# A four-tap convolution on two halves of TensorE's rows: no shifted copies of k, and another listed order

## The chip, the cores and the metric

The kernel runs on one core of a Trainium2 chip. A core has TensorE (PE, with its weight loads as PEld), VectorE (DVE), ScalarE (ACT), GpSimd (POOL) and SyncE (SP), and 16 DMA engines. The metric is the device time of one execution in microseconds (us), taken as the median of several.

## The reference

All tensors have 2048 rows (time) and 640 columns (channels), in bf16. Part A is a long convolution with gates, part B a feed-forward network:

```python
k_shift = sum over t in 0..3 of k_pad[:, t:t + S, :] * shift_k[:, 3 - t]   # short convolution, 4 taps per channel
kv = k_shift * v
y = irfft(rfft(kv, 2S) * rfft(ssm_k, 2S))[:S] + kv * ssm_D                 # long convolution, per channel
h = x + layernorm(x) * y
out = h + (silu(layernorm(h) @ w_gate) * (layernorm(h) @ w_up)) @ w_down   # inner width 1728
```

The short convolution is what the change is about: each output of a channel is the sum of the current and the three rows before of `k`, each times a number of that channel.

## The kernel before

Time is cut into four blocks of 512 rows. Row `t` of a block lies on partition `t // 4` at slot `r = t % 4`. For each block `j` the stages, with the names that the plan gives them, are: `kj` (short convolution, times v, gives `kv`), `gj` (the block of `ssm_k` turned), `Gj` and `Xj` (spectra of `g` and `kv`: matmuls of line 388, taken out of PSUM by ACT or DVE at lines 377 and 380, sums on DVE at 423 and 452 to 464), `mij` (complex products on DVE, 789 to 818), `nj` and `ij` (layernorm sums on ACT at 829 and 876; inverse transform, matmuls of line 960, and the gate on DVE), `tj` (the second layernorm, turned to `hT`), and `fj` (the feed-forward network: gate and up projections, matmuls of line 1184 into 128 x 512 outputs, then the down projection, line 1077).

The last 64 of the 1728 inner columns are the `tail`: `last_chunk` (1089) multiplies 64 partitions at a time, alternating between partitions 0 to 63 and 64 to 127.

The short convolution is done by matmuls whose stationary operand is a 128-channel slab of turned `k` (channels on partitions, time along it), and whose moving operand is a diagonal matrix of tap values; their sum over the taps is the output with time on partitions.

- Block 0: `k` is loaded plainly, turned by TensorE (629, taken out at 633) into four arrays by slot, and multiplied with 128-wide diagonals `diag`, one for each tap and slab: 80 matmuls of 128 columns (661).
- Blocks 1 to 3: `load_two` (565) loads `k` turned by DMA (576) into half of the tile `T`. Three more moves (`put`, 580; each of 64 partitions, by ACT at 584 or by DMA at 582) build arrangements in which partitions 64 to 127 hold the same 64 channels as partitions 0 to 63, moved in time. So one 128-row matmul with a 64-wide pair of stacked diagonals (`pairs`) does two taps of 64 channels: 80 matmuls of 64 columns a block (670).
- The taps are turned by TensorE (1341, 1358). DVE and POOL fill `diag` (1349), POOL fills `pairs` (1371).
- An output is taken out of PSUM slot by slot, four times a block: by DVE straight with the product by v (680), or by ACT (686) with DVE's product after it (687).

The program's order is written out by hand. Every operation is numbered as it is added to a plan; `ORDER` (77) lists the numbers. Each engine, and each DMA queue (SP's and POOL's), does its operations in that order. A negative number `-n-1` takes the other way given for operation `n`: an eviction or a product on DVE in place of ACT, or a sum by an accumulating DMA from POOL's queue (`add_into`, 284, and `or_add`, 289, which records line 292) in place of DVE. `SLOTS` gives the number of buffers of each kind; one buffer of `ps` is a pair of PSUM banks, and there are four for all uses. `spin` (1328) puts matmuls with no use in front of work to come.

Of the kernel before, what the change touches and what calls it, by code (L numbers as in the profile page):

```python
# [17 lines left out]
D = 640  # L18
# [53 lines left out]
TWOTAPS = True  # L72
TWONS = 640
# [147 lines left out]
def kernel(ctx: ExitStack, tc: tile.TileContext, A_q, A_k, A_v, A_shift_k, A_ssm_k, A_ssm_D, B_x,  # L221
# [90 lines left out]
    WF = fixed([P, R, 4, P], BF16, "WF")  # L312
    WI = fixed([P, 4, R, P], BF16, "WI")
    taps = fixed([P, 4 * KT], FP32, "taps")
    diag = new("diag") if TWOTAPS else fixed([P, KT * 4, P], BF16, "diag")
    if TWOTAPS:
        T = fixed([P, 2 * KT * TW], BF16, "T")
        taps2 = fixed([P, 4 * KT], FP32, "taps2")
# [219 lines left out]
    def window_of(gT, prev):  # L538
# [22 lines left out]
        return H  # L561

    H2 = P // 2

    def load_two(j):

        t = tk
# [961 lines left out]
```

## Time and profile before

| what | us |
|---|---|
| median of 3 executions | 258.9 (258.63 to 259.22) |
| the profiled execution | 258.74 |
| its span in the profile | 257.0 |
| PE busy | 248.3 |
| DVE busy | 199.8 |
| ACT busy | 176.8 |
| POOL busy | 74.0 |

The profile's span begins and ends a little inside the execution. The granted clock of TensorE is full in all slices. A matmul's duration in a row is longer than its spacing in a row of matmuls, since they are pipelined; spacings are taken from the chain of waits (pieces of work and their time) or from merged rows of the timeline (start, time, engine, line, operation, count).

### The profile page before, as it was taken

To read this page: it belongs to the slowest core of one execution; us is meant where nothing else is said; L and a number is where in the kernel's file an instruction comes from. 1 tells how busy PE (TensorE), PEld (TensorE's weight loads), DVE (VectorE), ACT (ScalarE), POOL (GpSimd) and SP (SyncE) were. 2 spreads that over 40 slices of the span, in tenths; PEclk is the share of its full clock that TensorE was granted. 3 is DMA by queue.
4 is the path that set the end of the run, shared out by engine and by line. 5 is a ranking of instruction groups with operands and counts; after the bars stand their busy time and mean duration, and the time that the engine had idled before them with its cause. 6 is when DMAs were issued, how large, how long until landed. Compare 5 with 4: busy or idle time off the path is not lost.

```text
span 257.0 us, 4668 instructions
## 1 busy us (share of the span) xinstructions
PE 248.3 (97%) x1802; PEld 149.8 (58%) x1802; DVE 199.8 (78%) x283; ACT 176.8 (69%) x297; POOL 74.0 (29%) x98
## 2 busy tenths in 40 slices
PE   7899997999999999999999999999999999999994
PEld 7786765654444876664445776544456754444662
DVE  3889999999999999999999999999999300001313
ACT  2499999977997995884586987976687244452400
POOL 5864105111111303427014211369940023000000
PEclk9999999999999999999999999999999999999999
DMA  6999999899896898999997989969690317000002
GB/s 215 379 213 281 264 212 353 205 189 261 196 182 220 139 235 131 191 218 194 192 238 134 219 202 143 218 149 211 172 270 4 77 26 101 3 0 0 0 28 77
DMA packets 54720, 43.31 MB, mean 169 GB/s; under 512 B 25605, under 2 KB 48970, under 8 KB 54698
## 3 DMA queue, kind: packets, MB, share of 16 engines
q1 hardware_dynamic: 48000, 28.58, 44.6%
q0 software_dynamic: 6688, 14.43, 30.7%
q8 instruction: 14, 0.23, 0.4%
q14 instruction: 8, 0.07, 0.1%
q10 hardware_dynamic: 10, 0.01, 0.0%
HBM read 23.99 MB, written 4.59 MB: 111 GB/s over the span
## 4 chain that ended last, share of the span: by engine, by line
PE 80%; ACT 9%; DMA 3%; DVE 3%; issue 2%; SPq 1%; POOL 0%; ACTq 0%; DVEq 0%
PE ps L1184 45%; PE ps L1077 23%; PE ps L388 5%; PE ps L960 4%; DMA big<-in_A_q_dram 3%; ACT big L377 2%; PE ps L670 2%; ACT row L829 2%; ACT row L876 2%; ACT S L377 1%; ACT big L488 1%; DVE row L971 1%; DVE big L974 1%; DVE big L687 0%; ACT big L686 0%
## 5 line engine op out<-in xcount | busy, mean ns | idle before, releaser
L1184 PE MATMUL ps<-big,big 128*128 128x512 bf16 x540 | 118.4, 379 | 0.0
L1184 PEld LDWEIGHTS <-big 128*128 128x128 bf16 x540 | 52.8, 98 | 62.2 <-issue 0.4
L1077 PE MATMUL ps<-wd,tT 128*128 128x320 bf16 (+2 forms) x416 | 59.0, 299 | 0.0
L1077 PEld LDWEIGHTS <-tT 128*128 128x128 bf16 x416 | 40.2, 98 | 16.9 <-issue 1.3
L1176 ACT ACTIVATE tT<-ps 128x1024 bf16<-128x1024 f32 x24 | 24.6, 1025 | 21.5 <-PE ps L1184 21.3
L388 PE MATMUL ps<-big,WF 128*128 128x320 bf16 x224 | 36.7, 298 | 1.2 <-ACT big L377 0.7
L817 DVE TENSOR_TENSOR big<-S,S 128x2560 bf16<-128x2560 bf16 x24 | 35.3, 1490 | 0.0
L1174 ACT CAST co<-ps 128x1024 bf16<-128x1024 f32 x24 | 23.8, 1010 | 11.9 <-PE ps L1184 11.6
L388 PEld LDWEIGHTS <-WF 128*128 128x128 bf16 x224 | 21.2, 97 | 11.5 <-issue 2.8
L292 POOL DMA_DIRECT2D S<-big x11 | 13.9, 1263 | 48.3 <-DVE big L817 15.4
L1178 DVE TENSOR_TENSOR tT<-tT,co 128x2048 bf16<-128x2048 bf16 x12 | 14.5, 1223 | 15.7 <-ACT co L1174 15.7
L818 DVE TENSOR_TENSOR S<-S,big 128x2560 bf16<-128x2560 bf16 x17 | 25.2, 1488 | 0.1
L829 ACT ACTIVATE row<-big 128x640 bf16<-128x640 bf16 x32 | 23.4, 740 | 1.1 <-DMA big<-in_A_q_dram 0.6
L887 ACT ACTIVATE row<-big,sm 128x640 bf16<-128x640 bf16 x22 | 19.6, 924 | 3.0 <-DVE sm L865 3.0
L1113 POOL DMA_DIRECT2D out_dram<-row x12 | 13.0, 1530 | 25.7 <-ACT row L1112 25.7
L1196 DVE TENSOR_TENSOR tT<-tT,co 128x512 bf16<-128x512 bf16 x4 | 1.7, 424 | 21.7 <-ACT co L1195 21.7
L377 ACT CAST S<-ps 128x640 bf16<-128x640 f32 (+1 forms) x27 | 15.0, 613 | 1.3 <-PE ps L388 1.3
L1112 ACT CAST row<-ps 128x640 bf16<-128x640 f32 x12 | 7.8, 696 | 10.0 <-PE ps L1077 8.9
L377 ACT ACTIVATE big<-ps 128x640 bf16<-128x640 f32 (+1 forms) x26 | 14.7, 617 | 0.0
L582 POOL DMA_DIRECT2D T<-T x5 | 5.2, 1039 | 25.5 <-DMA T<-in_A_k_dram 10.0
L851 POOL TENSOR_TENSOR sm<-sm 128x4 f32<-128x4 f32 x4 | 7.2, 1790 | 18.4 <-ACT row L876 18.4
L789 DVE TENSOR_TENSOR big<-S,S 128x2560 bf16<-128x2560 bf16 (+1 forms) x10 | 12.2, 1224 | 0.0
(111 smaller groups left out, 316.7 us busy)
## 6 DMA issues: line engine op xcount, KB each, us to landing
S<-big POOLq DMA_DIRECT2D x9, 640.0 KB, 6.6
big<-in_B_w_gate_dram SPq DMA_DIRECT2D x14, 320.0 KB, 5.3
big<-in_B_w_up_dram SPq DMA_DIRECT2D x11, 320.0 KB, 4.8
big<-in_A_ssm_k_dram SPq DMA_DIRECT2D x4, 640.0 KB, 5.7
big<-in_A_q_dram SPq DMA_DIRECT2D x4, 640.0 KB, 7.1
big<-in_A_v_dram SPq DMA_DIRECT2D x4, 640.0 KB, 6.1
wd<-in_B_w_down_dram SPq DMA_DIRECT2D x1, 2080.0 KB, 11.8
out_dram<-big SPq DMA_DIRECT2D x3, 640.0 KB, 3.4
```

Of the source, the lines that this page charges most:

```text
L292: op.other = ("add", P * n * 2 / 1280 * plan.TOOK[1280] / 16 * 2.1, lambda: nc.gpsimd.dma_start(out=to(), in_=what(), accum_op=ALU.add, ma ...
L377: (lambda: nc.scalar.activation(dst(), src(), ACT.Copy, scale=2.0)) if twice else (lambda: nc.scalar.copy(dst(), src())),
L388: nc.tensor.matmul(ap(ps)[:, h, 0:NH], w, ap(src)[:, r, h * NH:(h + 1) * NH], start=(first and i == 0), stop=(last and i == len(rs) - 1), ...
L817: dve(1490, lambda b=b, xs=xs, hs=hs: nc.vector.tensor_mul(flat2(b), X.part(xs), H.part(hs)), [X.at(xs), H.at(hs)], [b], [A.b])
L818: dve(1490, lambda b=b, dst=dst, f=f: f(A.part(dst), A.part(dst), flat2(b)), [b], [A.at(dst)])
L829: act(825, lambda r=r, junk=junk: nc.scalar.activation(ap(junk), ap(x)[:, r, :], ACT.Square, scale=D ** -0.5, accum_out=sm(s, 1)[:, r:r + ...
L887: nc.scalar.activation(ap(row), ap(x)[:, r, :], ACT.Identity, bias=sm(s, 5)[:, r:r + 1], scale=sm(s, 4)[:, r:r + 1])
L1077: nc.tensor.matmul(to, t, w, skip_group_check=True, **flags)
L1174: act(1010, lambda ps=ps: nc.scalar.copy(ap(co)[:, at:at + 2, :], ap(ps)), src, [(co, gi % 2)])
L1176: act(1010, lambda ps=ps: nc.scalar.activation(ap(tT)[:, c:c + 2, :], ap(ps), ACT.Silu), src, [done(range(c, c + 2), ROWS)])
L1178: dve(1220, lambda: nc.vector.tensor_mul(ap(tT)[:, c - 2:c + 2, :], ap(tT)[:, c - 2:c + 2, :], ap(co)), [co], [done(range(c - 2, c + 2), R ...
L1184: nc.tensor.matmul(ap(ps)[:, i, :], ap(w)[:, k, off:off + P], ap(hT)[:, k, :], start=(k == 0), stop=(k == KT - 1))
```

## The change

All four blocks now take one way, `by_halves`:

- `T` holds one turned copy of `k`, five slabs of 512 times with a pad of 16 in front. The three times before a block are copied there by POOL. Blocks 1 to 3 are loaded by the same four DMA transposes a block (`load_rows`). Block 0 is loaded to a buffer of its own (one more `big` buffer), turned by TensorE as before, and its evictions write every fourth element of `T`.
- The 64-wide diagonals now carry one tap: `pairs[p, t, c, e]` is the tap `t` of channel `128 c + p` where `p % 64 == e`, and zero elsewhere. All are made by one DVE product; one POOL addition makes the two stacked identities. The tiles `diag` and `taps2`, their fills and the second turning of the taps are gone, and so are all `put` moves.
- A block has three groups: slabs 0 and 1, slabs 2 and 3, slab 4. For each time offset `at` from -3 to 3 and each slab there are two matmuls, one on partitions 0 to 63 and one on 64 to 127, into two PSUM banks. The stationary operand is a strided window of `T`; the moving operand holds the diagonals of all slots to which this window contributes: 256 columns for `at = 0`, 192, 128 and 64 columns for 1, 2 and 3 steps away. This makes 14 matmuls and 2048 columns a slab, 70 matmuls and 10240 columns a block.
- An output is taken out group by group, three times a block, of 1024, 1024 and 512 columns; DVE's product by v follows in the same cut. The transforms of line 388 wait for column groups of `kv` instead of slots.

`ORDER` is new throughout. What it lists, decoded by counting the operations:

- First loads on SP's queue: before WF, g0, k0, x0, (a tail of w_down), v0; now (that tail), k0, g0, x0, v0, WF.
- On TensorE ahead of the first projection of `f0`: before 24 of the 32 matmuls of `X1` (line 388), with the other 8 behind the first two projections; now all 32. Of the removed setup's two spins of four matmuls, one now stands ahead of `f0` and one ahead of `X2`.
- On ACT ahead of the last step of `t0`: the layernorm sums `n1` (8 rows of lines 829 and 876) are now behind it. Evictions for DVE and ACT are dealt out anew.
- Convolutions: block 2 has its groups in three places apart (ahead of `i1`, ahead of the down projection of `f0`, in it); block 3 in two places.
- the 32 matmuls of `X2` are now followed at once by the 32 of `G3`, between `f0` and `f1`; before, `X2` lay among the last chunks of `f0`, and two projections of `f1` stood between.
- Three sums that were on DVE (two of 128 x 2560, one of 128 x 640) become accumulating DMAs.

```diff
+    if TAPROWS:
+        T = fixed([P, KT * TW], BF16, "T")
+        ident2 = fixed([P, P // 2], BF16, "ident2")
+        pairs = fixed([P, 4 * KT, P // 2], BF16, "pairs")
...
+    def load_rows(j):
+        plan.add("pool", 500, lambda: nc.gpsimd.tensor_copy(tk()[:, :, PAD - 3:PAD], tk()[:, :, TW - 3:TW]), [of_t(*[(R - 1, r) for r in range(1, R)])], [of_t("halo")])
+        for a in range(R):
+            transfer(MB / 4, lambda a=a: nc.sync.dma_start(
+                out=tk()[:, :, PAD + a * P:PAD + (a + 1) * P], in_=kk[j * BLK + a * P:j * BLK + (a + 1) * P, :], transpose=True),
+                [], [of_t(*[(a, r) for r in range(R)])])
...
+    def by_halves(kv, v, behind):
+        for i in range(3):
+            cs = range(2 * i, min(2 * i + 2, KT))
+            ps = conv_ps()
+            def mm(cs=cs, ps=ps):
+                for at in (0, 1, -1, 2, -2, 3, -3):
+                    r0, r1 = max(0, at), min(R - 1, R - 1 + at)
+                    for c in cs:
+                        for b in range(2):
+                            rows = slice(b * H2, b * H2 + H2)
+                            nc.tensor.matmul(ap(ps)[:, b, 0:len(cs) * R * H2].rearrange("p (r c e) -> p r c e", r=R, e=H2)[:, r0:r1 + 1, c - cs[0], :], tk()[rows, c, PAD + at:PAD + at + BLK - 3:R],
+                                             ap(pairs).rearrange("p (t c) e -> p t c e", c=KT)[rows, r0 - at:r1 - at + 1, c, :],
+                                             start=(at == 0), stop=(abs(at) > 1), skip_group_check=True)
...
+            op = plan.add("act", 1010 if n > 1 else 590, lambda to=to, src=src: nc.scalar.copy(to(), src()), [ps, v], [(kv, f"w{i}")], (),
+                          ("dve", 1230 if n > 1 else 690, straight))
+            op.rest = (dve(690 if n > 1 else 420, lambda cols=cols: nc.vector.tensor_mul(cols(ap(kv)), cols(ap(kv)), cols(rd(v))), [v], [(kv, f"w{i}")]),)
...
+    if TAPROWS:
+        plan.add("pool", 350, lambda: nc.gpsimd.tensor_tensor(ap(ident2), ap(ident)[:, 0:P // 2], ap(ident)[:, P // 2:P], op=ALU.add), [ident], [ident2])
+        dve(1480, lambda: nc.vector.tensor_mul(ap(pairs), ap(ident2).unsqueeze(1).broadcast_to([P, 4 * KT, P // 2]), ap(taps).unsqueeze(2).broadcast_to([P, 4 * KT, P // 2])), [ident2, taps], [pairs])
+    for _ in range(SPINS[0] if TAPROWS else 0):
+        spin(4)
-SLOTS = {'S': 8, 'big': 12, 'kT': 0, 'tT': 1, 'row': 5, 'sg': 0, 'co': 2, 'ps': 4, 'sm': 6}
+SLOTS = {'S': 8, 'big': 13, 'kT': 0, 'tT': 1, 'row': 5, 'sg': 0, 'co': 2, 'ps': 4, 'sm': 6}
```

More of the change, by code (lines that the diff above doesn't have):

```diff
@@ L72 @@
 TWOTAPS = True
+TAPROWS = True
 TWONS = 640
@@ L314, with tk @@
     taps = fixed([P, 4 * KT], FP32, "taps")
-    diag = new("diag") if TWOTAPS else fixed([P, KT * 4, P], BF16, "diag")
-    if TWOTAPS:
+    if TAPROWS:
+        T = fixed([P, KT * TW], BF16, "T")
+        ident2 = fixed([P, P // 2], BF16, "ident2")
+        pairs = fixed([P, 4 * KT, P // 2], BF16, "pairs")
+        def tk():
+            return ap(T).rearrange("p (c t) -> p c t", c=KT)
+        TOKENS = tuple((a, r) for a in range(R) for r in range(R))
+    else:
+        diag = new("diag") if TWOTAPS else fixed([P, KT * 4, P], BF16, "diag")
+    if TWOTAPS and not TAPROWS:
         T = fixed([P, 2 * KT * TW], BF16, "T")
@@ L389, in mm @@
                                      start=(first and i == 0), stop=(last and i == len(rs) - 1), skip_group_check=True)
-        pe(136 * len(ws) * len(rs), mm, [(src, x) for r in rs for x in (r, f"{r}w", f"{r}n")] + [WF] + ([(m, "f")] if m else []) + ([] if first else [ps]), [ps], holds)
+        pe(136 * len(ws) * len(rs), mm, [(src, x) for r in rs for x in (r, f"{r}w", f"{r}n")] + [(src, f"w{i}") for i in range(ws[0], ws[-1] + 2)] + [WF] + ([(m, "f")] if m else []) + ([] if first else [ps]), [ps], holds)
     def wide(n, ws):
@@ L621, in turned_k @@
             return k
-        src = rd if plan.block else plain
+        src = rd if plan.block or TAPROWS else plain
         kT = T if TWOTAPS else new("kT")
@@ L633, in turned_k @@
             evict(lambda copy, r=r, pt=pt: copy(
-                tk0()[:, :, r, 1:] if TWOTAPS else ap(kT)[:, :, r, PAD:], turned(pt)[:, 0:D].rearrange("p (c t) -> p c t", c=KT)),
-                [pt], [of_t(("K", r)) if TWOTAPS else (kT, r)], other=490)
+                tk()[:, :, PAD + r:PAD + r + BLK - 3:R] if TAPROWS else tk0()[:, :, r, 1:] if TWOTAPS else ap(kT)[:, :, r, PAD:], turned(pt)[:, 0:D].rearrange("p (c t) -> p c t", c=KT)),
+                [pt], [of_t(*[(a, r) for a in range(R)]) if TAPROWS else of_t(("K", r)) if TWOTAPS else (kT, r)], other=490)
             if table:
@@ L640, in kv_of @@
     def kv_of(j, kT, before, v, behind=None):
+        if TAPROWS:
+            if j == 0:
+                dve(60, lambda: nc.vector.memset(tk()[:, :, PAD - 3:PAD], 0.0), [], [of_t("halo")])
+            kv = new("t4")
+            by_halves(kv, v, behind)
+            return kv
         two_taps = TWOTAPS and j > 0
@@ L690, in kv_of, with src, cols, to @@
         return kv
+    def by_halves(kv, v, behind):
[11 more added lines that the diff above has]
+                                             start=(at == 0), stop=(abs(at) > 1), skip_group_check=True)
+            n = len(cs)
+            op = pe(530 * n + 190, mm, [of_t("halo", *TOKENS), pairs], [ps], [kv], 258)
+            if behind:
+                op.deps.add(behind)
+            def src(ps=ps, n=n):
+                return ap(ps)[:, :, 0:n * R * H2].rearrange("p b (r c e) -> p r c b e", r=R, e=H2)
+            def cols(t, cs=cs):
+                return t[:, :, cs[0] * P:(cs[-1] + 1) * P]
+            def to(cols=cols):
+                return cols(ap(kv)).rearrange("p r (c b e) -> p r c b e", b=2, e=H2)
+            def straight(to=to, src=src, cols=cols):
+                nc.vector.tensor_mul(to(), src(), cols(rd(v)).rearrange("p r (c b e) -> p r c b e", b=2, e=H2))
+            op = plan.add("act", 1010 if n > 1 else 590, lambda to=to, src=src: nc.scalar.copy(to(), src()), [ps, v], [(kv, f"w{i}")], (),
+                          ("dve", 1230 if n > 1 else 690, straight))
+            op.rest = (dve(690 if n > 1 else 420, lambda cols=cols: nc.vector.tensor_mul(cols(ap(kv)), cols(ap(kv)), cols(rd(v))), [v], [(kv, f"w{i}")]),)
     def by_rows(kv, v):
@@ L1345 @@
     dve(170, lambda: nc.vector.tensor_copy(ap(taps), ap(pt)[:, 0, 0:4 * KT]), [pt], [taps])
-    for c in range(KT):
+    if TAPROWS:
+        plan.add("pool", 350, lambda: nc.gpsimd.tensor_tensor(ap(ident2), ap(ident)[:, 0:P // 2], ap(ident)[:, P // 2:P], op=ALU.add), [ident], [ident2])
+        dve(1480, lambda: nc.vector.tensor_mul(ap(pairs), ap(ident2).unsqueeze(1).broadcast_to([P, 4 * KT, P // 2]), ap(taps).unsqueeze(2).broadcast_to([P, 4 * KT, P // 2])), [ident2, taps], [pairs])
+    for c in () if TAPROWS else range(KT):
         def fill(c=c, v=nc.vector if c < DIAGDVE else nc.gpsimd):
@@ L1367 @@
     fills = []
-    for c in range(KT if TWOTAPS else 0):
+    for c in range(KT if TWOTAPS and not TAPROWS else 0):
         def fill2(c=c):
```

6 lines of the change are left out of this document (4 added, 2 removed), and 77 rows, old and new, of the table ORDER.

## The prediction

> **What bounds the kernel now.** The page's first lines, then its chain of waits in order of time (start, us, what).
>
> ```profile
> span 257.0 us, 4668 instructions
> PE 248.3 (97%) x1802; PEld 149.8 (58%) x1802; DVE 199.8 (78%) x283; ACT 176.8 (69%) x297; POOL 74.0 (29%) x98
> ...
> 50.07 0.44 PE ps L1020 x5
> 50.51 2.17 PE ps L388 x16
> 52.68 2.16 PE ps L1184 x10
> 54.84 1.09 PE ps L388 x8
> ...
> 103.07 0.29 PE ps L388 x2
> ...
> 103.98 0.69 ACT row L1112
> ...
> 143.52 2.63 PE ps L670 x80
> ...
> 253.67 0.42 DVE row L1123
> ```
>
> From 50.07 on the chain is matmuls to the end, but for 1.3 us from 103.36 to 104.67. So what follows the first projection at 52.68 is worth its time on PE: 253.67 - 52.68 = 200.99 us. Ahead of it, another thing rules. The windows (us, then busy time and count of PE, PEld, DVE, ACT, POOL, granted clock, DMA share):
>
> ```profile
> 8.94:51.68 42.74, 39.67 (x434) 30.08 (x435) 40.89 (x79) 41.40 (x95) 16.97 (x34) 1.00 1.06 265
> 50.07:253.67 203.60, 203.28 (x1305) 114.64 (x1304) 156.11 (x187) 135.38 (x203) 51.78 (x51) 1.00 0.70 146
> ```
>
> In 8.94 to 51.68 ACT and DVE are busy for 41.40 and 40.89 of 42.74 us, and the 434 matmuls there are worth some 36 us at their spacings (some 168 of 320 columns at 0.136 us, 186 of 128 at 0.056, 80 of 64 at 0.033, from rows here and below): PE waits for evictions and sums. So I cost the change twice: the start by the work of ACT and DVE and by when they can begin, the rest by PE's work alone.
>
> **The convolution on PE.** A row of 80 old matmuls of 64 columns takes 2.63 us, 32.9 ns each. The other spacings, and the only matmuls that already run on half of the rows, from the timeline and the groups:
>
> ```profile
> 13.56 2.40 PE L661 MATMUL ps<-big,T 128*128 128x128 bf16 x40
> ...
> 89.11 12.12 PE L1077 MATMUL ps<-wd,tT 128*128 128x320 bf16 x88
> 101.16 0.72 PE L1077 MATMUL ps<-wd,tail 64*128 64x320 bf16 x8
> 101.81 1.26 PE L1077 MATMUL ps<-wd,tT 128*128 128x320 bf16 x8
> ...
> L661 PE MATMUL ps<-big,T 128*128 128x128 bf16 x80 | 5.0, 219 | 0.0
> L1077 PEld LDWEIGHTS <-tail 64*128 64x128 bf16 x32 | 1.2, 94 | 1.6 <-issue 1.3
> ```
>
> 128 columns: (2.40 - 0.219) / 39 = 56 ns. 320 columns: (12.12 - 0.30) / 87 = 136 ns. The tail's eight matmuls of 320 columns, on rows 0 to 63 and 64 to 127 in turn, take 101.81 - 101.16 = 0.65 us; one after another they would take 1.09, in pairs 0.54. So the halves run side by side, and going in and out of them costs: 12.70 us from 89.11 to 101.81, less 88 x 0.136 and 4 x 0.136, leaves 0.19.
>
> A pair then costs what one matmul of its width does. Between 2.5 ns and the column time (56 at 128, 136 at 320: 0.417 ns a column), 256 columns cost 109 ns, 192 83, 128 56, and 64 take the measured 33. A slab: 109 + 2 x (83 + 56 + 33) = 453 ns; five slabs 2.26 us. Block 2 has three visits: 2.26 + 3 x 0.19 = 2.83. Block 3 has two: 2.64. Together 5.47 against 2 x 2.63: **+0.2 us**. If the narrow pairs are held by two loads of 33 ns each (66 for 128 and 64 columns), a slab costs 539 ns and the sum is +1.1. If the halves didn't overlap at all, 5 x 2 x 453 = 4.53 a block and +4.7. I take +0.2, since the tail is the nearest row.
>
> The Trainium skill ("TensorE: Matmul & The Clock Gate", section "The mechanism") speaks against it: a weight load goes ahead of a running matmul only where the row groups differ. Read strictly, each pair would wait for its load; the tail's eight in 0.65 us don't show that. What it would make here is the third rival.
>
> The spin of four matmuls now ahead of `X2` costs 4 x 56 ns: **+0.2 us**. Eight matmuls of line 388 that stood behind the start of `f0` now stand ahead of it: **-1.1 us** (the chain's 1.09 at 54.84).
>
> **The start.** When data comes, and what ACT and DVE can do then:
>
> ```profile
> 0.80 0.35 SPq L1386 DMA_DIRECT2D WF<-const_wf  x1
> 1.20 0.50 SPq L343 DMA_DIRECT2D big<-in_A_ssm_k_dram  x1
> 1.75 0.52 SPq L616 DMA_DIRECT2D T<-in_A_k_dram  x1
> 2.31 0.59 SPq L355 DMA_DIRECT2D big<-in_A_q_dram  x1
> ...
> 7.06 0.75 PE L486 MATMUL ps<-ident,big 128*128 128x128 bf16 x10 [1.11 <-DMA big<-in_A_ssm_k_dram]
> 8.94 0.69 ACT L488 COPY big<-ps 128x640 bf16<-128x640 bf16 x1 [0.73 <-PE ps L486]
> 8.98 1.12 PEld L629 LDWEIGHTS <-T 128*128 128x128 bf16 x20 [0.24 <-DMA T<-in_A_k_dram]
> 11.30 0.74 ACT L829 ACTIVATE row<-big 128x640 bf16<-128x640 bf16 x1 [0.57 <-DMA big<-in_A_q_dram]
> 12.03 0.72 ACT L876 ACTIVATE row<-big 128x640 bf16<-128x640 bf16 x1
> 17.65 0.82 DVE L680 TENSOR_TENSOR big<-ps,big 128x640 bf16<-128x640 f32 x1
> 49.53 0.49 DVE L1022 COPY big<-ps 128x640 bf16<-128x640 bf16 x1
> 50.32 1.36 ACT L1022 COPY big<-ps 128x640 bf16<-128x640 bf16 x2
> ```
>
> Before, WF (512 KB) is first, and g0, k0 and x0 (640 KB each) are there at 7.0, 9.0 and 11.3: some 2 us for 640 KB. With WF sixth, k0 lands at about 5.8, g0 at 7.5, x0 at 9.6, v0 at 11.7, WF at 13.4 (estimates at that rate). ACT then takes out three pieces of k0 (0.69 each) from 6.3 to 8.4, and five rows of `n0` (0.72 apart) from 9.6 to 13.2, 5.7 us of work by 13.4; before, it had done two evictions and three rows, 3.5 us. It is **2.2 to 2.5 us ahead**, and waits little for the late WF.
>
> What ACT has to do ahead of `hT` stays nearly the same. By the lists: eight rows of `n1` less (-5.8), two k0 evictions more and one of g0 less (+0.7), three halves of spectra (half of 0.705 each, +1.1), two of g1 and g2 (+1.4), three of `X1` (+2.1), the kv of block 1 as 1010 + 1010 + 586 ns instead of three of 700 (+0.5), `t0` as four evictions instead of two and one row of L887 (+0.4); sum +0.4. The rows:
>
> ```profile
> L1174 ACT CAST co<-ps 128x1024 bf16<-128x1024 f32 x24 | 23.8, 1010 | 11.9 <-PE ps L1184 11.6
> L1195 ACT CAST co<-ps 128x512 bf16<-128x512 f32 x4 | 2.3, 586 | 4.1 <-PE ps L1184 4.1
> L686 ACT CAST big<-ps 128x640 bf16<-128x640 f32 x10 | 6.8, 705 | 0.0
> L887 ACT ACTIVATE row<-big,sm 128x640 bf16<-128x640 bf16 x22 | 19.6, 924 | 3.0 <-DVE sm L865 3.0
> L680 DVE TENSOR_TENSOR big<-ps,big 128x640 bf16<-128x640 f32 x6 | 4.9, 824 | 0.9 <-PE ps L661 0.7 <-ACT S L377 0.2
> L687 DVE TENSOR_TENSOR big<-big,big 128x640 bf16<-128x640 bf16 x10 | 4.7, 484 | 0.0
> L380 DVE TENSOR_SCALAR big<-ps 128x320 bf16<-128x320 f32 x6 | 2.8, 480 | 0.0
> L423 DVE TENSOR_TENSOR S<-big,S 128x2560 bf16<-128x2560 bf16 x3 | 4.5, 1491 | 0.0
> L1349 DVE TENSOR_SCALAR big<-ident,taps 128x128 bf16<-128x128 bf16 x16 | 3.2, 295 | 0.1
> L584 ACT COPY T<-T 64x2570 bf16<-64x2570 bf16 x3 | 7.0, 2332 | 0.1
> ```
>
> DVE: its 16 fills go (3.2 us), and one product of 1280 elements comes. The trace has none; the bounds are 0.97 (twice 484, L687) and 1.65 (twice 824, L680). I take 1.5, nearer L680, since one operand is fp32; it runs at about 7 to 8.5 ahead of g0's evictions. kv of block 0 is taken out by DVE in pieces of 1024, 1024 and 512: with 824 for 640, 1.29 ns an element bounds it above, 1.32 + 1.32 + 0.66 = 3.3, as much as the four old ones. v0 at 11.7 lets it end at about 15; before, the last one ended at 18.47. From there to the last step of `t0` DVE took 49.53 + 0.49 - 18.47 = 31.55. Its list for this stretch now has four halves of spectra more (L380, +1.9), the sum of `G2` (L423, +1.5), two evictions of g less (-1.0), block 1 as three products (some 0.7 + 0.7 + 0.4) instead of one L680 and three L687 (-0.5), and four rows of `t0` for three and two evictions (-0.5): +1.4. So it is done at 15 + 33.0 = 48.0. A turn and one eviction by ACT (0.45 and 0.69) make `hT` whole at 49.1; before, 50.32 + 1.36 = 51.68. That is -2.6, and ACT's side says -2.2 to -2.5. Last, `f0` stood 1.0 behind `hT` for 16 matmuls of `X1`; now one transform (0.54) follows the last turn. The start of `f0` moves from 52.68 to about 49.7: **-3.0 us**, bounds 0 and -5 (when DVE and ACT both gain what they save and wait for nothing).
>
> Costs that lie under others: evictions of k0 that write every fourth element (0.49 on DVE; 0.82 if they run as L680 does; one is on DVE's list, under the wait for g0); POOL's addition and halo copies, in place of 24 fills and five moves (POOL is busy for 29%); DMA transposes of k for block 1 behind the convolution of block 0 (at about 13 instead of 10.31), while the convolution of block 1 came at 40.58. SP's loads for `f0` queue behind them, three of 0.5 to 1.4 us.
>
> **The rest.** ACT loses 7.0 us of copies and gets `n1` (5.8) where it was busy for 135 of 204 us; DVE loses three sums to POOL's queue, which loses five of T's moves. These buy nothing on PE. `X2` and `G3` in one run hold 64 matmuls, 8.7 us, with 13 evictions on ACT (9.2 us at L686's 0.705) and one of L1112 ahead of them: PE waits 0.5 to 1.5 us there, about the 1.3 at 103.4 that it replaces. The step on DVE that closes the kernel is the same.
>
> **Sum.** 258.74 (profiled) - 3.0 - 1.1 + 0.2 + 0.2 = 255.0; the median lies 0.16 above the profiled execution: 255.2.
>
> **Rivals.**
> 1. The start isn't freed: ACT and DVE wait at 9 to 14 for WF and v0, or for the order. `f0` starts at 52.7 as before, and only -1.1 + 0.4 is left: 258.2. For it: DMA's share is 1.06 in 8.94 to 51.68, so loads may come later than at my rate. Against: T's moves leave that queue.
> 2. More: the start gains 5, or the 1.3 us hole goes too: 252.8 to 253.5.
> 3. The other side: halves don't overlap as in the tail. It has one place (2 x 70 matmuls behind 50 us) and decides from 2 x 1.85 us, where it eats the 3.7 gained. With the two halves of a pair one after another: 255.2 + 4.5 = 259.7. With each pair waiting for its load (94 ns, the tail's group): 7 x 94 a slab, 3.3 a block: 255.2 + 6.6 = 261.8. For it: strided loads and widths under 320 columns aren't shown on half rows. Against: the tail.
> 4. PE runs dry in the run of `X2` and `G3` or behind an accumulating DMA for more than 4 us: 259 and up. For it: DVE has no idle time there; against: it has less work than before.
>
> **Chances.** Forecast 0.58, first rival 0.16, second 0.10, third 0.10, fourth 0.06. A difference of 0.2%, 0.5 us, is what a measurement of this kernel can tell. Faster: the forecast but for 0.03, the second rival, and half of the first: 0.73. Same: the other half of the first and 0.02: 0.10. Slower: 0.17. The range leaves out some of the second rival and the dear half of the third: 252.8 to 259.7.
>
> **What would show it.** The convolution's line: pairs 3 or 4 ns apart, some 2.3 to 2.7 us a block without its visits (4.5: third rival). The first row of L1184 at 49.7 (at 52 or later: first rival). Behind it a chain of matmuls, with at most 2 us of ACT or DVE between `f0` and `f1` (more: fourth). The forecast is wrong if that first row is early and the end isn't.

## The result, and the profile after

The changed kernel takes 257.09 us (median of 4 executions, 256.87 to 257.41) where the kernel before takes 258.76 us beside it: a ratio of 0.9937, with an interval of 0.9914 to 0.996. It is faster, but by 1.7 us and not by the 3.7 us that the forecast's sum gave. A later set gave 257.19 against 258.64 us, 0.9938 (0.9921 to 0.9956). The profiled execution took 256.92 us.

The page's first lines and, below them, the chain of waits of the kernel after (start, us, what):

```profile
span 254.8 us, 4492 instructions
PE 246.5 (97%) x1758; PEld 146.3 (57%) x1758; DVE 194.6 (76%) x256; ACT 173.5 (68%) x295; POOL 60.0 (24%) x71
...
1.44 4.21 DMA big<-in_A_k_dram
...
6.19 1.59 ACT T L652
...
7.82 0.44 PE ps L648 x5
8.26 0.94 PE ps L1394 x16
9.20 0.57 PE ps L495 x10
...
12.67 1.74 DVE big L747 x2
...
50.58 0.70 PE ps L397 x4
51.28 27.05 PE ps L1244 x125
...
78.33 1.03 PE ps L729 x28
79.36 1.19 PE ps L1244 x5
...
81.63 1.08 PE ps L1244 x5
...
85.97 0.57 PE ps L729 x13
...
100.45 1.03 PE ps L729 x28
...
103.34 0.83 DVE S L389
...
125.16 1.48 PE ps L729 x40
...
127.83 1.03 PE ps L729 x28
...
251.73 0.56 DVE row L1183
```

The lines have moved: 397 is the transform's matmul (388 before), 386 and 389 its evictions (377, 380), 1244 the gate and up projections (1184), 652 the evictions of the turned block 0 of `k` (633), 495 and 497 the turning of `g` and its evictions, 729 the convolution (661 and 670), 747, 748 and 750 the three ways of taking it out, 944 a row of `t0` on DVE (947 on ACT), 1080 and 1082 the turning of such a row and its eviction (1020, 1022), 1020 the inverse transform (960), 1031 its gate on DVE (971), 432 a sum of spectra (423), 1394 the spins. Runs that load or turn `k` in another way have these a few lines further on.

The kernel falls into the same two parts as before. From the first projection to the last row's start it took 251.73 - 51.28 = 200.45 us, where the forecast had 200.3 (200.99 - 1.1 + 0.2 + 0.2). That part came out, in part by luck, as is told below. The first projection starts at 51.28, where the forecast had 49.7. That is 1.4 us earlier than before, not 3.0, and nearly the whole error lies there.

The chain shows where to look. It now begins with `k` of block 0 and an eviction of 1.59 us, for which the last turn of `k` waits (7.82); sixteen spins and the turning of `g` follow that turn on PE. The groups of the evictions, of the kernel before and then after (busy us, mean ns of one, idle time ahead):

```profile
L633 DVE COPY T<-ps 128x640 bf16<-128x640 bf16 x3 | 1.4, 491 | 0.2 <-PE ps L629 0.2
L633 ACT COPY T<-ps 128x640 bf16<-128x640 bf16 x1 | 0.7, 692 | 0.4 <-PE ps L629 0.4
```

```profile
L652 ACT COPY T<-ps 128x640 bf16<-128x640 bf16 x3 | 4.5, 1666 | 3.3 <-PE ps L648 3.3
L652 DVE COPY T<-ps 128x640 bf16<-128x640 bf16 x1 | 1.6, 1579 | 3.4 <-PE ps L648 3.4
L1408 DVE TENSOR_TENSOR pairs<-ident,taps 128x1280 bf16<-128x1280 bf16 x1 | 1.5, 1516 | 0.0
L747 DVE TENSOR_TENSOR big<-ps,big 128x1024 bf16<-128x1024 f32 x3 | 3.6, 1210 | 0.1
L748 ACT CAST big<-ps 128x1024 bf16<-128x1024 f32 x5 | 5.3, 1066 | 0.4 <-PE ps L729 0.3
```

The same 640 bf16 elements from PSUM take 1579 ns on DVE instead of 491, and 1666 on ACT instead of 692. What differs is that they now go to every fourth element of `T`, in steps of 8 bytes. The last two rows are the new evictions of the convolution; they (1210 and 1066 ns for 1024 elements) and the product of the diagonals (1516 ns) took about what the forecast gave them (1.32 and 1.01 us, 1.5 us).

### The profile page after: what moved, and what is told of

Same layout as the page of the kernel before. It is cut to its first block, busy times and chain, and to the rows that moved or that the text cites. A ratio compares the mean times of both kernels' runs of the same rounds, so it can differ in the third digit from the quotient of the medians.

```text
span 254.8 us, 4492 instructions
## 1 busy us (share of the span) xinstructions
PE 246.5 (97%) x1758; PEld 146.3 (57%) x1758; DVE 194.6 (76%) x256; ACT 173.5 (68%) x295; POOL 60.0 (24%) x71
## 4 chain that ended last, share of the span: by engine, by line
PE 84%; ACT 8%; DVE 4%; DMA 2%; issue 1%; SPq 0%; DVEq 0%
PE ps L1244 46%; PE ps L1137 24%; PE ps L397 6%; PE ps L1020 4%; PE ps L729 3%; ACT big L386 3%; ACT S L386 2%; DMA big<-in_A_k_dram 2%; DVE big L1034 1%; PE ps L495 1%; ACT big L497 1%; ACT big L1082 1%; DVE big L747 1%; ACT row L889 1%; DVE row L1031 1%
## 5 line engine op out<-in xcount | busy, mean ns | idle before, releaser
L1137 PE MATMUL ps<-wd,tT 128*128 128x320 bf16 (+2 forms) x416 | 58.4, 299 | 0.0
L397 PE MATMUL ps<-big,WF 128*128 128x320 bf16 x224 | 36.0, 298 | 1.7 <-ACT big L386 0.4
L1236 ACT ACTIVATE tT<-ps 128x1024 bf16<-128x1024 f32 x24 | 24.5, 1024 | 17.4 <-PE ps L1244 17.4
L1234 ACT CAST co<-ps 128x1024 bf16<-128x1024 f32 x24 | 23.9, 1012 | 12.8 <-PE ps L1244 11.2
L292 POOL DMA_DIRECT2D S<-big x13 | 15.2, 1173 | 55.7 <-DVE big L849 24.8
L878 DVE TENSOR_TENSOR S<-S,big 128x2560 bf16<-128x2560 bf16 x16 | 23.7, 1486 | 0.1
L947 ACT ACTIVATE row<-big,sm 128x640 bf16<-128x640 bf16 x20 | 17.7, 920 | 6.8 <-DVE sm L925 6.8
L386 ACT ACTIVATE big<-ps 128x640 bf16<-128x640 f32 (+1 forms) x29 | 16.8, 622 | 0.0
L575 POOL COPY T<-T 128x15 bf16<-128x15 bf16 x3 | 4.6, 1525 | 33.2 <-PE ps L729 33.2
L849 DVE TENSOR_TENSOR S<-S,S 128x2560 bf16<-128x2560 bf16 (+1 forms) x10 | 12.1, 1219 | 0.0
L1020 PEld LDWEIGHTS <-WI 128*128 128x128 bf16 x96 | 9.2, 98 | 4.8 <-DMA big<-in_B_w_up_dram 0.2
```

Source lines behind the costliest of these rows:

```text
L386: (lambda: nc.scalar.activation(dst(), src(), ACT.Copy, scale=2.0)) if twice else (lambda: nc.scalar.copy(dst(), src())),
L397: nc.tensor.matmul(ap(ps)[:, h, 0:NH], w, ap(src)[:, r, h * NH:(h + 1) * NH], start=(first and i == 0), stop=(last and i == len(rs) - 1), ...
L849: return lambda: f(*(x() for x in args))
L878: dve(1490, lambda b=b, dst=dst, f=f: f(A.part(dst), A.part(dst), flat2(b)), [b], [A.at(dst)])
L947: nc.scalar.activation(ap(row), ap(x)[:, r, :], ACT.Identity, bias=sm(s, 5)[:, r:r + 1], scale=sm(s, 4)[:, r:r + 1])
L1020: nc.tensor.matmul(ap(ps)[:, w, 0:NH], m, src[:, w * NH:(w + 1) * NH], start=(i == 0), stop=(i == len(terms) - 1))
```

## The experiments

None of them leaves out a part of the computation; the one that runs a block's matmuls twice writes the same values twice. Each has the kernel before beside it on the same chip, and the ratios are to that; the kernel after itself was run again only in the fourth set. Cuts in the code are marked by dots.

### First set: the stepped evictions, and the convolution's price

Theory: the evictions in steps of 8 bytes hold back T, and with it the start. Rivals: the loads bound the start, or the convolution costs more than thought.

**Evictions in a row, smaller packets.** Block 0 of `k` is loaded so that a slot's 128 times are neighbours, and the eviction writes 128 elements in a row.

```diff
+load(MB, 1280, lambda: nc.sync.dma_start(out=rd(b), in_=kk[0:BLK, :].rearrange("(r p) d -> p r d", p=P)), [b])
...
-tk()[:, :, PAD + r:PAD + r + BLK - 3:R] if TAPROWS
+tk()[:, :, PAD + r * P:PAD + (r + 1) * P] if TAPROWS
```

> The changed kernel, but block 0 of k is loaded so that partition p holds the times p, 128 + p, 256 + p and 384 + p (packets of 1280 bytes instead of 5120); turned, a piece is 128 times in a row, and its eviction writes T without steps. Nothing else changes. Theory (the four stepped evictions of k0, 1.58 to 1.72 us each instead of 0.69 on ACT and 0.49 on DVE, ate the start's gain): the evictions fall to about 0.7 and 0.5, T is whole 2 us earlier than 10.65, the first projection moves from 51.28 to about 49.8, the time falls by 1.2 to 1.6 us. Rival (the start is held by the list: the last turn of t0 stands behind transforms of X1 that wait for ACT, or by late loads): the evictions get shorter, the first projection moves by less than 0.4 and the time by less than 0.5 us.

256.66 us (256.07 to 257.52), 0.9913 (0.9885 to 0.9942). The groups:

```profile
L657 ACT COPY T<-ps 128x640 bf16<-128x640 bf16 x3 | 1.9, 694 | 4.2 <-PE ps L653 4.2
L657 DVE COPY T<-ps 128x640 bf16<-128x640 bf16 x1 | 0.5, 492 | 4.3 <-PE ps L653 4.3
```

The durations are those of before again, so the step is what made them long. But `k` took 5.14 us to land in this execution where it had taken 4.21, and `f0` came at 50.59, 0.7 us sooner than after and about half of what was expected. The smaller packets aren't shown to be the cause: in a later run with the same packets `k` took 4.5 us, and in one with the long ones 5.1.

**No turns and no evictions.** Block 0 comes by four DMA transposes, as the other blocks do.

```diff
+for a in range(R):
+    nc.sync.dma_start(out=tk()[:, :, PAD + a * P:PAD + (a + 1) * P], in_=kk[a * P:(a + 1) * P, :], transpose=True)
...
```

> The changed kernel, but block 0 of k comes into T by four DMA transposes as blocks 1 to 3 do; the four turns on TensorE and their evictions are left out, and the list is kept otherwise. Theory (the start is bound by the work of ACT and DVE): ACT loses 5.1 us and DVE 1.58 us ahead of 10.65; if the transposes land by about 9 the first projection comes 1.5 to 2.5 us earlier and the time falls by as much. Rival (loads rule the start): the transposes hold SP's queue for some 5 us ahead of g0, x0, v0 and WF, these land as much later, and the time rises by 1 to 3 us.

261.23 us (260.15 to 262.29), 1.0087 (1.0057 to 1.0117). The timeline of SP's queue:

```profile
0.80 0.58 SPq L1525 DMA_DIRECT2D wd<-in_B_w_down_dram  x1
1.44 5.25 SPq L622 DMA_TRANSPOSE T<-in_A_k_dram  x4
6.73 0.58 SPq L352 DMA_DIRECT2D big<-in_A_ssm_k_dram  x1
```

Four transposes hold the queue for 5.25 us, 1.3 each. The load of `g0` is issued at 6.73 us instead of 2.06, and the others follow it; `g0` landed at 11.66 and `f0` started at 55.08. The rival holds here: the loads decide once they are late enough.

**Block 3's convolution twice.**

```diff
+times = 2 if plan.block == 3 else 1
...
-for at in (0, 1, -1, 2, -2, 3, -3):
+for at in (0, 1, -1, 2, -2, 3, -3) * times:
```

> The changed kernel, but every matmul of block 3's convolution is issued a second time in the same group (the second pass starts the sums anew, so the output stays). Theory (behind the first projection only PE's own work counts, and a half-row matmul costs 37 ns on average): 70 more matmuls cost 2.5 to 2.7 us of time, and the gap between f0 and f1 doesn't change. Rival (DVE or ACT set the pace there, PE has slack): less than 1.3 us. If the halves of a pair ran one after another the cost would be 4.5 us.

259.43 us (259.06 to 260.68), 1.0027 (1.0008 to 1.0045), 2.3 us above the kernel after. Its chain:

```profile
125.35 2.85 PE ps L730 x84
...
129.39 1.94 PE ps L730 x51
```

140 matmuls (the trace lacks a few) in 4.79 us: 34 ns each. Their mean width is 10240 / 70 = 146 columns, which at the 0.417 ns a column of the prediction would be 61 ns one after another. So the two halves do run side by side, and a block's 70 matmuls cost the 2.3 us that the forecast used, a little less than the 2.5 to 2.7 expected here.

**The step alone, in the kernel before.** Its four arrays by slot are laid out with the slot innermost, so that its evictions write in steps of 8 bytes. The matmuls of line 661 then read their stationary operand with that step; they keep their pace (2.40 us for a row of 40, as in the kernel before). All else is the kernel before.

```diff
-return ap(T)[:, KT * TW:KT * TW + KT * R * (P + 1)].rearrange("p (c r t) -> p c r t", c=KT, r=R)
+return ap(T)[:, KT * TW:KT * TW + KT * R * (P + 1)].rearrange("p (c t r) -> p c r t", c=KT, r=R)
```

> The kernel before, but its four arrays of turned k0 are laid out with the slot innermost, so that each eviction writes every fourth element; the matmuls of line 661 read their stationary operand with that step. Theory (a stepped eviction costs 1.6 to 1.7 us instead of 0.49 on DVE and 0.69 on ACT, and ACT and DVE bound the start): three on DVE cost 3.3 us and one on ACT 1.0 us more, the convolution of block 0 comes 1.5 to 3 us later, and the time rises by 1 to 3 us. Rival (it is hidden under the waits for x0 and v0): the evictions get longer and the time rises by less than 0.5 us.

261.39 us (260.86 to 263.21), 1.0101 (1.0063 to 1.0139). Its groups, and then its start of `f0` in the chain, which was at 52.68:

```profile
L633 DVE COPY T<-ps 128x640 bf16<-128x640 bf16 x3 | 4.5, 1621 | 0.1
L633 ACT COPY T<-ps 128x640 bf16<-128x640 bf16 x1 | 1.6, 1590 | 0.3 <-PE ps L629 0.3
```

```profile
54.85 2.16 PE ps L1184 x10
```

The same 1.6 us an eviction on both engines, in the other kernel, and 2.2 us at the start of `f0`.

### Second set: the step on the other side, and the early chain of DVE

**Step on the side that is read.** The load keeps its long packets. A slab's four slots are turned into one PSUM tile; the eviction reads with a step and writes 512 or 1024 elements in a row.

```diff
+slabs = ((0, 1), (1, 2), (2, 3), (3, 5))[r]
...
-tk()[:, :, PAD + r:PAD + r + BLK - 3:R], turned(pt)[:, 0:D].rearrange("p (c t) -> p c t", c=KT)
+tk()[:, slabs[0]:slabs[1], PAD:PAD + BLK].rearrange("p c (t r) -> p c t r", r=R),
+turned(pt)[:, 0:(slabs[1] - slabs[0]) * BLK].rearrange("p (c r t) -> p c t r", r=R, t=P)
```

> The kernel after, but the step of block 0 of k is put on the side that the evictions read: each slab of k0 is turned slot by slot into one PSUM tile, and the eviction reads the four slots with a stride and writes 512 or 1,024 times in a row into the SBUF array. The load keeps its packets of 5,120 B. Theory (the write in steps of 8 bytes is what makes an eviction 1.58 to 1.72 us): the evictions come back to 0.6 to 1.0 us, k0 still lands at 5.7 us, T is whole near 9.3 instead of 10.65, f0 starts at 49.9 to 50.5 instead of 51.28, and the time falls by 0.8 to 1.4 us against the kernel after, more than with the smaller packets. Rival (a stepped read costs what a stepped write costs): the evictions stay above 1.5 us and the time is the kernel after's within 0.3.

256.93 us (256.39 to 257.34), 0.9921 (0.9897 to 0.9945). Groups, then the first transforms in the timeline:

```profile
L656 ACT COPY T<-ps 128x512 bf16<-128x512 bf16 x2 | 1.2, 588 | 0.0
L656 ACT COPY T<-ps 128x1024 bf16<-128x1024 bf16 x1 | 1.0, 1012 | 3.7 <-PE ps L652 3.7
L656 DVE COPY T<-ps 128x512 bf16<-128x512 bf16 x1 | 0.7, 690 | 3.7 <-PE ps L652 3.7
```

```profile
13.81 2.47 PE L397 MATMUL ps<-big,WF 128*128 128x320 bf16 x15 [1.09 <-DMA WF<-const_wf]
```

A step on PSUM's side costs little on ACT: 1012 ns for 1024 elements, where 640 in steps on the SBUF side had taken 1666. On DVE it isn't free, with 690 ns for 512 elements where 640 in a row take 491. But the start did not move (51.29): `kv` of block 0 was ready 1 us sooner, and PE then waited 1.09 us for WF, whose transfer took 10.07 us in this execution against 8.7 to 9.1 in the others. Why it took longer here isn't known, and since the six times lie close together (256.39 to 257.34; this execution took 256.98), it isn't shown that this one is an exception. The time that the theory gave was missed.

**The product of the diagonals first.** On DVE it goes ahead of the eviction of `k`, into idle time.

```diff
-  ... 17, 24, 7, 22, -26, ... 14, 23, 15, 9, 47, ...
+  ... 17, 24, 7, 9, 22, -26, ... 14, 23, 15, 47, ...
```

> The kernel after with one step moved: VectorE makes the product of block 1's pairs before it evicts its part of block 0 of k, in the time in which it idles for that block. Theory (VectorE's own early chain holds a part of what is missing at f0's start): its part of kv0 begins 1 to 1.5 us sooner and f0 starts at 50.0 to 51.0 instead of 51.28, time down by 0.3 to 1.3 us. Rival (the pairs land too late for it, or the x side ends last anyway): f0 starts at 51.28 within 0.3, and the time doesn't move; if the product has to wait for the pairs, T is later and the time rises by up to 1 us.

257.61 us (257.0 to 257.76), 0.9943 (0.9922 to 0.9965); `f0` at 51.52, with `k` landing 0.27 us later than in the kernel after. The rival holds: DVE's order there decides nothing while T is late.

**Together with four spins for sixteen.** Once with the smaller packets, once with the step on the side that is read; both have the product first and four spins ahead of `g0`'s turning.

```diff
-WARMUP = (18, 16, 16)
+WARMUP = (18, 16, 4)
```

> Block 0 of k loaded in smaller packets and written in a row, the product of the pairs first on VectorE, and the sixteen spins ahead of g0's turn cut to four. Theory (the gains add): kv0 ends at 14.0 to 14.5, f0 starts at 49.6 to 50.3, time 255.5 to 256.2. Rival (x0's and g0's landing bound the start, not the work on k0): as with the smaller packets alone, f0 at 50.6 and 256.5 to 256.9.

> The step on the read side of block 0's evictions, the product of the pairs first on VectorE, and four spins in place of sixteen ahead of g0's turn. Theory (the three gains add): f0 starts at 49.3 to 50.0, time 255.0 to 255.8, which is what was forecast for the change itself. Rival (the loads bound the start): f0 at 50.3 or later, 256.2 or more.

256.12 us (255.84 to 257.84), 0.9901 (0.9872 to 0.9929), and 256.10 us (255.9 to 258.24), 0.9905 (0.987 to 0.994). In the chains `f0` starts at 50.17 and 50.16, so most of the gain is there, but 0.5 us short of the forecast's 49.7. The chain of the second begins elsewhere, and DVE's timeline has a wait where `kv` of block 0 is taken out:

```profile
3.70 8.82 DMA WF<-const_wf
...
12.57 4.11 PE ps L397 x26
```

```profile
11.35 2.95 DVE L752 TENSOR_TENSOR big<-ps,big 128x512 bf16<-128x512 f32 x3 [0.46 <-DMA big<-in_A_v_dram]
```

With the evictions out of the way, WF, which the change puts sixth, is what the first transforms wait for, and DVE waits 0.46 us for `v`. The first run lies within what its theory gave, near the end of it; the second lies between theory and rival. The forecast's "waits little for the late WF" was true only because something else was later.

### Third set: what paces the stretch up to `f0`

From DVE's first eviction of a spectrum (line 389) to the start of `f0` the kernels agree to 0.1 us:

| kernel | first eviction at | `f0` at | between |
|---|---|---|---|
| after | 15.47 | 51.28 | 35.81 |
| smaller packets | 14.87 | 50.59 | 35.72 |
| step on the side read | 15.58 | 51.29 | 35.71 |
| product first | 15.72 | 51.52 | 35.80 |
| all, smaller packets | 14.47 | 50.17 | 35.70 |
| all, step on the side read | 14.45 | 50.16 | 35.71 |

So this stretch is a chain that moves as one. In it ACT idles for 0.91 us, in the timeline of after: `G1`'s transform stands on PE behind matmuls of `i0`.

```profile
35.70 0.69 ACT L386 CAST S<-ps 128x640 bf16<-128x640 f32 x1 [0.91 <-PE ps L397]
```

Theory: ACT paces it, and the idle time can be won. Rival: DVE does. The transform (operation 209, with the eviction 208) is moved ahead of eight of `i0`'s twelve matmuls there, or of four, and one run with eight moved has all the earlier parts of the second set too.

```diff
-  ... 142, 206, 396, 198, 148, 141, 208, 147, 397, 146, 209, 199, 153, ...
+  ... 142, 206, 396, 198, 148, 208, 209, 141, 147, 397, 146, 199, 153, ...
```

> The kernel after with one step moved on TensorE: of G1's two transforms that stand behind the twelve matmuls of i0 at 32.2 us, the first now stands behind the first four of them. ACT idles 0.91 us at 34.79 for it. Theory (ACT paces the start of f0: in six kernels it came 36.96 to 37.17 us after ACT's first eviction of a spectrum): the idle 0.91 goes, f0 starts at 50.4 to 50.7 instead of 51.28, time down by 0.6 to 0.9 us. Rival (DVE paces it as well, since it has no idle time there and now gets i0's matmuls 0.5 us later): f0 starts at 51.28 or up to 0.5 later, time the same or up.

> The read-side step of block 0's evictions, the product of the pairs first, four spins for sixteen, and the same transform of G1 four matmuls behind the start of i0. Theory (gains add): f0 starts at 49.2 to 49.6, time 255.1 to 255.6, about what was forecast for the change. Rival (DVE paces the middle): f0 at 50.16 or later, 256.1 or more.

> The kernel after, with the same transform of G1 eight matmuls behind the start of i0 (of twelve) and not four. Theory (ACT paces): ACT's idle time falls from 0.91 to about 0.4, f0 starts 0.4 to 0.6 us sooner, time down by 0.3 to 0.6. Rival (DVE paces): DVE gets only the last four matmuls of i0 0.5 us later, so less harm than in the run with four: f0 within 0.3 of 51.28.

| kernel | median, us | ratio to before | first eviction to `f0` |
|---|---|---|---|
| ahead of eight matmuls | 258.18 (257.93 to 258.62) | 0.997 (0.9947 to 0.9992) | 36.73 |
| ahead of eight, with all earlier parts | 257.09 (256.87 to 257.27) | 0.9932 (0.9905 to 0.9959) | 36.64 |
| ahead of four matmuls | 257.79 (257.55 to 258.9) | 0.9953 (0.993 to 0.9976) | 36.35 |

All are slower than the same kernel without the move (257.09 and 257.19; 256.10 with all parts). Those ran on other chips, but the stretches up to `f0` are longer too, by 0.5 to 0.9 us. DVE's timeline in the first:

```profile
36.58 0.88 DVE L1031 SCALAR_TENSOR_TENSOR row<-big,sm,ps 128x640 bf16<-128x640 bf16 x1 [0.89 <-PE ps L1020]
```

DVE, which had no pause there, now has one of 0.89 us, and the stretch is 0.92 longer. With all parts it is again 0.89 and 0.93; with four matmuls moved the pause is 0.51 and the stretch 0.54 longer. The theory falls: at this place DVE paces, and ACT's idle time was spare.

**A row of `t0` on ACT** (-168 and 167 are the two ways of one operation).

```diff
-  ... 10, 399, 232, 236, -168, -171, ...
+  ... 10, 399, 232, 236, 167, -171, ...
```

> The kernel after with one row of t0's second layernorm (0.4 us on DVE) put on ACT, where such a row takes 0.92 us. Theory (ACT paces the start of f0): f0 starts 0.7 to 1.0 us later than 51.28, time up by 0.6 to 1.0. Rival (DVE paces it): f0 starts up to 0.4 us sooner, or stays within 0.2.

257.87 us (257.5 to 258.1), 0.9954 (0.9934 to 0.9975). The chain, then DVE's timeline:

```profile
46.80 0.80 ACT row L947
```

```profile
48.22 1.49 DVE L432 TENSOR_TENSOR S<-big,S 128x2560 bf16<-128x2560 bf16 x1 [1.15 <-ACT S L386]
```

The stretch takes 36.61 us, 0.80 more: just that row. DVE, which has a row of 0.4 us less to do, now waits 1.15 us for an eviction by ACT. So near the end of the stretch the pace has passed to ACT.

### Fourth set: the last leg, and the step by itself

**An eviction of `X1` given to DVE**, behind its last row of `t0`; alone, and together with the read-side step, the product first and the four spins.

```diff
-  ... 414, -165, 213, 169, 174, 212, 172, 224, 227, ...
+  ... 414, -165, -225, 213, 169, 174, 212, 172, 227, ...
```

> The kernel after with one of the X1 evictions that stand on ACT behind t0's last row (0.6 us) given to DVE, right behind its last row of t0. Theory (ACT's evictions pace the last leg, from t0's last row at 48.83 us to f0 at 51.28): f0 starts 0.5 to 0.6 us sooner, time down by 0.4 to 0.6. Rival (the last leg is the turns of t0 and their order on TensorE): f0 within 0.15 of where it was, no change.

> The read-side step, the product first, four spins for sixteen, and that X1 eviction on DVE. Theory (the gains add): f0 starts at 49.55 to 49.75, time 255.4 to 255.8. Rival (the last leg isn't ACT's): f0 at 50.1 to 50.3, 256.0 to 256.3.

**The kernel after again, and the step kept** with the product first and four spins.

> The kernel after, unchanged, as the measure for the other three on the same chip: f0 starts at 51.2 to 51.7, time 256.9 to 257.7.

> The kernel after with the product of the pairs first and four spins for sixteen, but with the evictions that write in steps of 8 bytes. Theory (these evictions are what delays kv0): f0 starts at 50.9 to 51.4, within 0.4 of the kernel after, and 0.7 to 1.2 later than with the step on the read side. Rival (the spins and the product's place made the gain of the two runs that had all parts): f0 at 50.1 to 50.4, time as theirs.

| kernel | median, us | ratio to before |
|---|---|---|
| `X1` eviction on DVE | 257.06 (256.81 to 257.77) | 0.9937 (0.9916 to 0.9957) |
| the same and the step on the side read | 256.20 (255.76 to 258.42) | 0.9918 (0.989 to 0.9947) |
| after, unchanged | 257.19 (256.81 to 257.44) | 0.9938 (0.9921 to 0.9956) |
| step kept, product first, four spins | 257.22 (256.98 to 259.11) | 0.9953 (0.9934 to 0.9972) |

The last two rows differ by 0.03 us, so with the step kept the spins and the place of the product win nothing. In the profiled execution of that kernel `f0` started only at 52.15, since `k` took 5.1 us to land there; its stretch is 35.81 us like that of the others. The first two rows differ in the read-side step, the product and the spins, and are 0.9 us apart; the second is 1.0 below the kernel after. The eviction of `X1` wins nothing by itself, so moving the step is worth about 1 us once the product and the spins are out of the way too; moved alone it had given 256.93 on the second set's chip, against 256.10 with them. How this interaction splits isn't settled, and since the intervals against the kernel before overlap, the 1 us rests on the medians of one chip and on the starts of `f0`. The three kernels without the stepped writes, with the product first and fewer spins (256.10 to 256.20), are the quickest that were found.

ACT's timeline in the kernel with that eviction of `X1` on DVE:

```profile
50.87 0.69 ACT L1082 COPY big<-ps 128x640 bf16<-128x640 bf16 x1 [0.41 <-PE ps L1080]
```

ACT now waits for the last turn of `t0`, which stands on PE behind a transform of `X1` that waits for DVE's eviction (0.83 us in the chain where ACT's took 0.60). `f0` starts at 51.61, against 51.50 in the kernel after beside it, and at 50.53 with the other parts. So the last leg is neither engine's alone: turns of `t0` and transforms of `X1` stand in turns on PE, and here a turn stood behind a transform that waited for an eviction. Whether another order of them would be shorter wasn't tried.

## Why the prediction was right in its direction and wrong in its size

**The sum, term by term** (time of the profiled execution):

| term | forecast | measured |
|---|---|---|
| start of `f0` | -3.0 (49.7) | -1.40 (51.28) |
| from there to the last row's start | -0.7 | -0.54 (200.99 to 200.45) |
| what lies outside | 0 | +0.12 |
| sum | -3.7 | -1.82 |

**The step that failed is the start's -3.0**, and in it the line "Costs that lie under others: evictions of k0 that write every fourth element (0.49 on DVE; 0.82 if they run as L680 does ...)", and 0.69 on ACT. They take 1.58 to 1.72 us. Both ends of the bound were too low: every row they came from writes its elements in a row, and the kernel before has no eviction that writes every fourth element. An operation that the trace doesn't show was priced by its count of elements, with no room for its pattern. The cover failed too: it was to lie "under the wait for g0", but the fourth turn of `k` waits for ACT's first eviction, and `g0`'s turning stands behind that turn and sixteen spins. With the step moved, the product first and four spins `f0` starts at 50.16 instead of 51.28, and the medians of one chip differ by 1.0 us.

In the forecast's own terms, the 1.58 us that are missing at `f0` are 0.53 at the end of `kv` of block 0, 0.3 in DVE's list behind it and 0.75 in the last leg. The first is less than the evictions cost, and that was luck: with the step alone moved, `kv` of block 0 was done at 11.62 + 2.94 = 14.56, sooner than the 15.0 of the forecast, so that an error the other way hid a part.

The Trainium skill ("SBUF — State Buffer", section "Door 1: The DMA port swizzle") says that SBUF has lines of 16 bytes, and that bf16 can therefore be stepped by up to eight elements for free. These writes step by four and cost 2.4 times (ACT) and 3.2 times (DVE) as much. The kernel before has one stepped read of SBUF by ACT, the copy of line 472: it reads every fourth element of the last block of `ssm_k` and writes in a row.

```profile
L472 ACT COPY big<-big 128x2560 bf16<-128x2560 bf16 x1 | 2.6, 2551 | 0.0
```

Its 2560 elements take 2551 ns, and 2570 in a row on 64 partitions take 2332 (line 584, in the prediction). So the measurement speaks against the rule for writes, and hardly for reads by ACT; no run here shows a stepped read of SBUF by DVE.

**The rest of the start.** The forecast had `kv` of block 0 done at 15.0 and `f0` 34.7 us behind it. It was done at 12.60 + 2.93 = 15.53, and at 11.35 + 2.95 = 14.30 in the kernel with all parts of the second set. The list of DVE's work was nearly right: 33.0 us forecast from there to the last row of `t0`, and 48.83 - 15.53 = 33.3 measured (both timelines below). What failed as well is the leg after it, forecast as a turn, one eviction and one transform, 1.7 us, and measured as 51.28 - 48.83 = 2.45. DVE and ACT, in the timelines of after:

```profile
12.60 2.93 DVE L747 TENSOR_TENSOR big<-ps,big 128x512 bf16<-128x512 f32 x3
...
48.39 0.44 DVE L944 TENSOR_SCALAR row<-big,sm 128x640 bf16<-128x640 bf16 x1
```

```profile
48.56 0.77 ACT L386 ACTIVATE big<-ps 128x640 bf16<-128x640 f32 x1
49.16 0.75 ACT L1082 COPY big<-ps 128x640 bf16<-128x640 bf16 x1
49.74 0.79 ACT L386 ACTIVATE big<-ps 128x640 bf16<-128x640 f32 x1
50.45 0.69 ACT L1082 COPY big<-ps 128x640 bf16<-128x640 bf16 x1
```

When the last row of `t0` was done, at 48.83, ACT had just begun on the last two evictions of each kind, which it does in turns. The forecast had added up the two engines' lists as if each ended when its own work was done.

**What held, and what came out by luck.** The eight matmuls of `X1` moved ahead (-1.1) and the spin (0.23 us in the chain) held, and the price of the new convolutions did: block 2 is 1.03 + 0.57 + 1.03 = 2.63 us in the chain and block 3 1.48 + 1.03 = 2.51, against 2.26 a block and 0.19 a visit. The chain's 28 matmuls of a group of two slabs in 1.03 us are 37 ns each. Each of the five visits shows as some 0.1 us more in the row behind it (1.19 for 1.08 at 79.36). That makes 5.67 us for the two blocks, where the forecast had 5.47.

But the term's difference, +0.2, was wrong, since the old convolution cost less in the chain than the 2 x 2.63 us that the forecast took off. In the kernel before (first the chain, then PE's timeline) 20 of block 2's 80 matmuls lay in the hole of 1.3 us, where PE waits anyway and the chain goes by other engines:

```profile
84.04 1.97 PE ps L670 x60
```

```profile
103.18 0.83 PE L670 MATMUL ps<-pairs,T 128*128 128x64 bf16 x20
```

So 1.97 + 2.63 = 4.60 us were freed, and the term is +1.1. It was made good by two gains that the forecast didn't have: the hole shrank from 1.3 to 0.9 us, and the matmuls of line 397 have 8.36 us in the chain behind `f0`, 1.40 less than those of 388 had, where 1.1 was forecast. That this part of the sum came out within 0.2 us is luck.

**The rivals.** The first (the start isn't freed) is half of what happened: less freed, but for another reason than late loads; its time, 258.2, didn't come. The loads came about as estimated (`k` at 5.65 us for 5.8). The second didn't come either: there is no gain past the forecast, though the hole did shrink by 0.4 us. The third is refuted: halves one after another would have made a block 4.5 us, and doubling a block would have cost that; it cost 2.3. On the strict reading of the Trainium skill ("TensorE: Matmul & The Clock Gate", section "The mechanism") each pair would wait for its load; the 37 ns don't show that. The fourth is refuted: between `f0` and `f1` the chain leaves PE for 0.83 us (the row at 103.34) and three issue times, 0.9 us, where it was 1.3.

## What to carry to other kernels

An eviction is priced by how it writes as much as by how many elements it writes: if a layout calls for a step, let the eviction read PSUM with the step and write SBUF in a row, which cost far less here. When a bound comes from rows of the trace, ask whether any of them has the new operation's access pattern; if none has, the bound isn't one from above. When old work is taken off, count only what of it lay on the chain. And where three engines take turns through a few buffers, a list that is as long as predicted still ends late if its last pieces alternate; and taking away idle time from an engine that doesn't pace can cost the one that does.

## What the runs showed of the hardware

- Writing 128 x 640 bf16 from PSUM to every fourth element of SBUF: 1.57 to 1.64 us on DVE, 1.57 to 1.74 on ACT. In a row: 0.49 and 0.69. A step on PSUM's side instead: 0.69 for 512 elements on DVE, 0.59 on ACT, and 1.01 for 1024 on ACT.
- A matmul whose stationary operand is read with that step keeps its pace: 2.40 us for 40 of 128 columns, with the step and without.
- Matmuls on 64 rows each, in pairs on the two halves of the rows, widths 64 to 256: 34 to 37 ns a matmul in rows of 28 to 84.
- At the start, issuing one DMA transpose of 128 rows of 640 bf16 holds SP's queue for 1.3 us (1.27 to 1.29), where a plain load of 640 KB holds it for 0.4 to 0.6. Later in the kernel after both can take longer, up to 2.6 and 2.1 us.
- The first large load, 640 KB of `k`, lands 4.1 to 4.7 us after its issue in most executions and 5.1 in two, one with packets of 1280 B and one with 5120 B. In the kernel after the start of `f0` moved with it (51.28 with 4.21, 51.50 with 4.42); with the step kept, the product first and four spins it was 52.15 with 5.11.
